# The first and the last of 64 recurrent steps rearranged: one segment's preparation between dense heads, stores in 4 KB runs, other queues, and output weights that stay in their slots

## The chip, the cores and the metric

The kernel runs on one core of a Trainium2 chip. The core has a matrix engine (TensorE, PE in the profile; PEld are its weight loads), a vector engine (DVE), a scalar engine (ACT), GpSimd (POOL) and a sync engine (SP) that does nothing here but issue DMAs. On-chip memory (SBUF) has 128 partitions; matmuls write to PSUM. The metric is device time of one execution in microseconds (us), lower is better. 16 DMA engines move all data between DRAM and SBUF; DMAs are issued on queues by SP, ACT and POOL.

## The reference

Two branches work on one layer-normalised input; their sum and the input make the output. All arrays are bfloat16.

```python
xn = _layernorm(x)                                   # x: 1 x 2048 x 1024
# branch A: memory-augmented recurrent attention, 64 segments of 32 rows, 32 heads of 128
mem = mem0                                           # 8 rows
for s in range(64):
    h = concat([mem, xn[:, 32*s:32*(s+1)]])          # 40 rows
    q, k, v = h @ Wq, h @ Wk, h @ Wv                 # each 1024 x 4096
    scores = where(mask, q @ k.T * scale, -1e9)      # per head, 40 x 40
    o = softmax(scores) @ v @ Wo                     # 4096 x 1024
    mem = o[:, :8]                                   # goes into the next segment
    outs.append(o[:, 8:])
# branch B: the two rows of xn with the largest xn @ w_r go through a gated MLP (F = 3584)
y = silu(x_sel @ w_gate) * (x_sel @ w_up) @ w_down * sigmoid(r_sel)
return x + concat(outs) + (xn + scatter(y))
```

The rows that carry memory make the 64 segments a chain: segment s+1 cannot begin before the output projection of segment s has given its 8 rows.

## The kernel before

**Split of the rows.** Each segment has 24 rows on which the next segment's memory depends, together with the 8 memory rows, and 8 rows that nothing waits for in the chain, called the left rows. The chain handles 32 rows per step (24 of x and 8 of memory). The left rows of all segments, 512 in all, have their q, k and v computed once, in the first step, with dense matmuls (`left_qk`, `left_v`), and their output projection once, after the last step (`left_rows_out`).

**Weights.** Wq, Wk, Wv and Wo are cut into 64 granules of 512 KB. 44 are resident in SBUF, one is held in two pieces, one in spare PSUM banks, and 18 (`streamed`) are read from DRAM in every step through a pool `wstream` of 5 slots (tile name `g`). The list `flow` holds the order of all such reads; `fetch` takes its head and issues it on SP. In the first step the reads come from the weight arrays; GpSimd also copies the streamed granules to scratch DRAM (`copy_block`, tiles `wsc`), from which later steps read. A step has six phases p = 0 to 5 (q, k, q, k, v, v for two halves of the heads; `PSm`, L699), and then 16 pieces of output projection (`WO`, L735). A table `hooks` puts small work (transposes, scores, softmax, attention) at a phase and a granule, here (5, 0) for the softmax of the second half.

**The first step.** `left_qk(mat, half, ...)` runs 16 heads, each of 8 matmuls (L477) and one ACT copy into `GA` (L479); it runs behind phases 0 to 3. For the first half's q its heads 0 to 7 run before the recurrent chain starts. Then come the mean and deviation of segment 0's rows (`spread(0, 1)`: PE L254, DVE L259 to L261), their normalising (`norm_seg(0)`, DVE L289 to L304), the transposes into the step's left operand `ST` (`new_st`, `mem_to_st`: PE L309, ACT L328, DVE L333), and the statistics of all other rows (`row_stats`, DVE L241/L242, tiles t = 1 to 15). Behind phase 0, `left_done(0)` needs these for `spread(1, NT)`, again L254 on PE. The gathered q and k of a half go to DRAM (`ql_d`, L490, on POOL). `left_v` runs behind phases 4 and 5: four blocks b of 128 left rows, each with four times 8 matmuls (L499) into `PSV`; ACT and DVE alternate in copying them to one of four slices of `VG` (L502), and SP stores each slice to `vl_d` (L503). A slice is written again by the next block, so its store must be done by then. `left_done(4)` loads eight output granules into one area, `W8B` (SP, L138). `GATE` is a four-column copy on POOL whose only role is to hold back the GpSimd copies behind it.

**Between steps.** `load_qkl` (L553, POOL) reads one segment's left q and k, 128 KB, from `ql_d` to the tile `QKL`.

**The last step and after.** The projection of the left rows needs all 16 output granules again (`WOS`): 11 are resident, and `flow` ends with five entries of a step 64 that read the five streamed ones (g = 49, 52, 56, 59, 62) once more. `left_rows_out(k)` makes two blocks with 64 matmuls each (`WD`, L809). The weights of branch B (tiles `MW`, 46 loads) go into homes that the last step frees (`fetch_moe`); `after(s, g)` issues one load behind each streamed output granule, and `gate_up` (`GU`, L871) and the last matmuls (`YP`, L895) use them.

The order on every engine is the order of the code; the pools only add waits.

Of the kernel before, what the change touches and what calls it, by code (L numbers as in the profile page):

```python
# [8 lines left out]
BF16 = mybir.dt.bfloat16  # L9
# [19 lines left out]
def kernel(  # L29
# [16 lines left out]
    nc = tc.nc  # L46
# [67 lines left out]

    ql_d = [dram.tile([2, 8, P, 256], BF16, name=f"ql_d{t}") for t in range(NSEG // 8)]
    vl_d = [dram.tile([16, 16, XL, 2, P], BF16, name=f"vl_d{t}") for t in range(4)]
# [18 lines left out]

    def load_resident(g):
        t = room(g, f"wres{g}")
        nc.sync.dma_start(out=granule_out(t, g), in_=granule_dram(g))  # L138
        res_tiles[g] = t
# [64 lines left out]
    RIL = MISC[:, 892:908].bitcast(F32).rearrange("p (t c) -> p t c", c=2)  # L204
    GATE = MISC[:, 908:912]

# [41 lines left out]
    def spread(t0, t1):  # L248

        n = t1 - t0  # L250
        sd_rows(MV[:, t0:t1, :], VE[:, t0:t1])
        PD = OPB
        for s in range(4):
            nc.tensor.matmul(PD[:, 32 * s:32 * s + 2 * n], lhsT=SELM[:, s, :, :].rearrange("p r g -> p (r g)"),  # L254
                             rhs=MV[:, t0:t1, :].rearrange("p t c -> p (t c)"),
                             start=(s == 0), stop=True, skip_group_check=True)
        for s in range(4):
            mr = MR.rearrange("p (t s) c -> p t s c", s=4)[0:XR4, t0:t1, s, :]
            nc.vector.tensor_copy(out=mr, in_=PD[0:XR4, 32 * s:32 * s + 2 * n].rearrange("p (t c) -> p t c", c=2))  # L259
        nc.vector.tensor_copy(out=RI16[:, t0:t1, 0], in_=MV[:, t0:t1, 0])  # L260
        nc.vector.reciprocal(out=RI16[:, t0:t1, 1], in_=MV[:, t0:t1, 1])  # L261
# [136 lines left out]
    flow += [(s, g) for s in range(NSEG) for g in (streamed if s else first_streamed)]  # L398
    flow += [(NSEG, g) for g in streamed if g >= 48]

# [69 lines left out]
    def left_qk(mat, half, Gs, between, h0=0, h1=16):  # L470
# [13 lines left out]
        if mat == 1:  # L484
            G3 = gathered[half]
            if half == 0:
                qkl[0] = one.tile([P, 2, 2, 4, 4, XL], BF16, tag="bA", name="QKL")
            nc.vector.tensor_copy(out=qkl[0][:, half].rearrange("p m i q r -> p (m i q r)"), in_=G3[:, 0, :])
            for k in range(NSEG // 4):
                nc.gpsimd.dma_start(out=ql_d[k // 2][half, 4 * (k % 2):4 * (k % 2) + 4].rearrange("s p c -> p s c"),  # L490
                                    in_=G3[:, 4 * k:4 * (k + 1), :])

    def left_v(half, Gs):
        VG = home(hm, [P, 2048], BF16, "VG")
        for b in range(4):
            for jq in range(4):
                PSV = psA.tile([P, 512], F32, tag="acc", name="PSV")
                for kc in range(KC):
                    nc.tensor.matmul(PSV[:, :], lhsT=XLT[:, kc, P * b:P * (b + 1)], rhs=part(Gs[kc], jq),  # L499
                                     start=(kc == 0), stop=(kc == KC - 1))  # L500
                VQ = VG[:, 512 * jq:512 * (jq + 1)]
                (nc.vector.tensor_copy if jq % 2 else nc.scalar.copy)(out=VQ, in_=PSV[:, :])  # L502
                nc.sync.dma_start(out=vl_d[b][4 * jq:4 * jq + 4, :, :, half, :].rearrange("i s r e -> (s r) i e"),  # L503
                                  in_=VQ.rearrange("p (i e) -> p i e", i=4))
            if b == 1:
                if half == 0:
# [3 lines left out]
    def left_done(p):  # L510
        for g in range(8 * p, 8 * (p + 1)):
            if g in first_streamed:
                fetch()
        if p == 0:
            spread(1, NT)
            for t in range(NT):
                router_tile(t)
            nc.gpsimd.tensor_copy(out=GATE, in_=gathered[0][:, 0, 0:4])
        elif p == 1:
# [9 lines left out]
        elif p == 4:  # L529
            area("big1", [P, 8, 2048], "W8B")  # L530
            for g in AREAS["big1"]:
                load_resident(g)
        elif p == 5:
# [7 lines left out]
    def after(s, g):  # L541
# [3 lines left out]
        if s == NSEG - 1:  # L545
            if g in resident and g < 48 and g not in place and g not in resident[:3]:
                free_homes.append(g)
            if g in streamed and g >= 48:
                fetch_moe(1)

    def load_qkl(s):
        t = qkl[0] = one.tile([P, 2, 2, 4, 4, XL], BF16, tag="bA", name="QKL")
        nc.gpsimd.dma_start(out=t.rearrange("p h m i q r -> p h (m i q r)"),  # L553
                            in_=ql_d[s // 8][:, s % 8].rearrange("h p c -> p h c"))

# [7 lines left out]
    qkl = [None]  # L563
    group = {}

    left_stats()
    left_turns()
    row_stats(xt(0), S6, MV[:, 0, :])
    left_qk(0, 0, [t for _, t in first_phase], iter(()), 0, 8)
    spread(0, 1)  # L570
    norm_seg(0)
    ST = new_st(0)
    mem_to_st(OB, ST)
    for t in range(1, NT):
        row_stats(xt(t), S6, MV[:, t, :])

    for s in range(NSEG):
# [108 lines left out]
        hook(4, 6, lambda: scores(1))  # L686
        hook(5, 0, exponent)
        hook(5, 0, lambda: soften(1))
        hook(5, 4, lambda: attend(0, 0))
# [52 lines left out]
        for w in range(16):  # L742
# [4 lines left out]
            if w == 2 and s + 1 == NSEG:  # L747
                OTA = area("big0", [P, NSEG, XL * H], "OTA")
                for k in range(8):
                    load_left_out(k, nc.gpsimd)  # L750
            Gv = granule(48 + w)
            project(WO, w, Gv, lhs_main, w == 15)
            if w == 9 and s + 1 < NSEG:
# [21 lines left out]
    for k in range(8, 16):  # L775
        load_left_out(k, nc.sync)
    WOS = {g: granule(g) for g in sorted(range(48, 64), key=lambda g: g in streamed)}
    XLS = [room(resident[k], "XLS") for k in range(2)]
# [158 lines left out]
```

## Time and profile before

| | |
|---|---|
| median of 3 runs | 1912.85 us (1912.07 to 1913.66) |
| the profiled execution | 1924.64 us, its span 1923.0 us |
| granted TensorE clock, mean | 0.977 |
| busy share of the span | PE 82%, PEld 43%, DVE 47%, ACT 40%, POOL 17% |
| moved by DMA | 672.39 MB, mean 350 GB/s |

The profile is of one execution; its time is 11.8 us above the median of the unprofiled runs. A row of a timeline gives start, duration, engine, line, operation, output<-input, shapes and count, and in brackets the idle time of that engine just before it and what ended it. A row of a view of stretches gives the stretch, its length, then for each engine busy time and number of instructions, the granted clock of PE (1.00 is full), the busy share of the 16 DMA engines and GB/s. A row of DMA issues gives output<-input, the queue, the count, the size of one, and the median time from its issue to its landing.

### The profile page before, as it was taken

The page shows a single profiled execution, that of the slowest core. Times are in us where ns is not written, and L with a number is a line of the kernel's source. Part 1 is how long each engine was busy: PE and PEld are TensorE (multiplying, and loading weights), DVE is VectorE, ACT ScalarE, POOL GpSimd, SP SyncE. Part 2 cuts the span into 40 slices and gives each one's busy share as a digit, 9 for nine tenths or more (in the row PEclk, how much of TensorE's full clock was granted, in tenths as well). Part 3 has the DMA queues.
Part 4 walks back from the last instruction along what each step waited for, and adds up shares of the span by engine and source line. Part 5 has one row for each costly group of instructions (what it writes and reads, how often), then busy time and mean ns, then how long its engine had stood idle before and what let it go on. Part 6 is the DMA issues. An engine that isn't in the chain of part 4 may idle for free. (4 is left out here: it accounts for less than half of the span.)

```text
span 1923.0 us, 70950 instructions
## 1 busy us (share of the span) xinstructions
PE 1574.8 (82%) x30354; PEld 821.4 (43%) x30378; DVE 907.3 (47%) x2774; ACT 768.4 (40%) x2018; POOL 329.1 (17%) x593
## 2 busy tenths in 40 slices
PE   6898778888888778888878888888887877888778
PEld 3444334444444434444444444444444444444455
DVE  5811245445555445444545555555444445555430
ACT  2342134444444444444434444444444444444400
POOL 1042011111111111111111111111111111111200
PEclk9999989999999999999999999999999999999988
DMA  9495699999999999999999999999999999999997
GB/s 364 185 337 168 191 357 363 371 366 375 374 361 381 338 358 375 371 356 366 382 352 357 376 371 376 370 377 375 365 366 365 357 370 365 375 375 367 369 343 278
DMA packets 234173, 672.39 MB, mean 350 GB/s; under 512 B 48192, under 2 KB 55664, under 8 KB 233856
## 3 DMA queue, kind: packets, MB, share of 16 engines
q1 hardware_dynamic: 208592, 621.96, 86.6%
q0 software_dynamic: 23248, 42.22, 6.7%
q8 instruction: 237, 3.88, 0.8%
q10 hardware_dynamic: 2016, 3.67, 0.6%
q14 instruction: 80, 0.66, 0.1%
HBM read 646.74 MB, written 29.76 MB: 352 GB/s over the span
## 5 line engine op out<-in xcount | busy, mean ns | idle before, releaser
L699 PE MATMUL PSm<-wres,ST 128*32 128x512 bf16 x6400 | 543.8, 389 | 22.9 <-DVE ST L333 22.9
L699 PEld LDWEIGHTS <-ST 128*32 128x32 bf16 x12288 | 305.7, 96 | 519.3 <-issue 203.9
L699 PE MATMUL PSm<-g,ST 128*32 128x512 bf16 x3332 | 338.4, 391 | 163.5 <-DMA g<-wsc 159.7
L708 ACT CAST XB<-PSm 128x512 bf16<-128x512 f32 x256 | 150.6, 588 | 279.6 <-PE PSm L699 276.7
L735 PEld LDWEIGHTS <-OT 128*32 128x32 bf16 x8192 | 204.8, 97 | 70.5 <-issue 55.9
L553 POOL DMA_DIRECT2D QKL<-ql_d x63 | 47.0, 746 | 978.8 <-DVE OTL L669 960.1
L598 DVE COPY KT<-BT 128x512 bf16<-128x512 bf16 x128 | 53.2, 415 | 258.1 <-PE BT L588 257.7
L735 PE MATMUL WO<-W8B,OT 128*32 128x256 bf16 x4096 | 162.6, 275 | 0.0
L699 PE MATMUL PSm<-W8A,ST 128*32 128x512 bf16 x2048 | 160.4, 386 | 0.0
L735 PE MATMUL WO<-g,OT 128*32 128x256 bf16 x2560 | 133.3, 278 | 17.8 <-DMA g<-wsc 14.6
L767 POOL DMA_DIRECT2D out_dram<-XN x256 | 128.9, 514 | 83.7 <-DVE XN L765 78.0
L390 DVE COPY g<-KEPT 128x512 bf16<-128x512 bf16 x126 | 53.5, 425 | 144.6 <-PE PSm L699 133.7
L377 ACT COPY BK<-KEPT 128x512 bf16<-128x512 bf16 x126 | 78.4, 622 | 104.6 <-PE WO L735 104.6
L716 ACT CAST VM<-PSm 128x512 bf16<-128x512 f32 x128 | 80.3, 627 | 76.6 <-PE PSm L699 76.6
L593 ACT COPY QT<-BT 128x512 bf16<-128x512 bf16 x128 | 75.1, 587 | 80.9 <-PE BT L588 46.6
L588 PEld LDWEIGHTS <-XB 128*128 128x128 bf16 x1024 | 58.3, 98 | 108.4 <-ACT XB L708 44.6
L588 PE MATMUL BT<-IDENT,XB 128*128 128x128 bf16 x1024 | 102.4, 223 | 0.0
L477 PE MATMUL PSG<-XLT,wres 128*128 128x512 bf16 x326 | 100.3, 382 | 1.5 <-ACT XLT L235 1.1
L615 DVE TENSOR_TENSOR BS<-BS,CT 128x96 f32<-128x96 f32 (+1 forms) x256 | 59.7, 233 | 86.7 <-PE BS L608 82.3
L596 ACT COPY KT<-QKL 128x128 bf16<-128x128 bf16 x128 | 38.4, 300 | 142.9 <-PE BT L588 105.5
L630 DVE TENSOR_REDUCE DN<-BS 128x8 f32<-128x320 f32 x128 | 62.9, 491 | 66.5 <-ACT BS L625 66.5
L294 POOL DMA_DIRECT2D XN<-in_A_x_dram x64 | 34.1, 533 | 296.6 <-PE PSm L699 212.7
(176 smaller groups left out, 2460.3 us busy)
## 6 DMA issues: line engine op xcount, KB each, us to landing
g<-wsc SPq DMA_DIRECT2D x950, 512.0 KB, 6.2
g<-wsc SPq DMA_DIRECT2D x126, 256.0 KB, 5.4
g<-wsc SPq DMA_DIRECT2D x63, 384.0 KB, 5.9
ql_d<-GA POOLq DMA_DIRECT2D x32, 256.0 KB, 7.2
QKL<-ql_d POOLq DMA_DIRECT2D x63, 128.0 KB, 5.5
MW<-in_B_w_gate_dram SPq DMA_DIRECT2D x16, 448.0 KB, 8.0
MW<-in_B_w_up_dram SPq DMA_DIRECT2D x16, 448.0 KB, 6.4
MW<-in_B_w_down_dram SPq DMA_DIRECT2D x14, 512.0 KB, 8.9
```

Of the source, the lines that this page charges most:

```text
L377: copy(out=back[c], in_=KEPT_COLS[KEPT_WHOLE][c])
L390: copy(out=t[:, 512 * c:512 * (c + 1)], in_=KEPT_COLS[g][c])
L477: nc.tensor.matmul(PSG[:, :], lhsT=part(Gs[kc], h // 4)[:, P * (h % 4):P * (h % 4 + 1)], rhs=XLT[:, kc, :], start=(kc == 0), stop=(kc == K ...
L588: nc.tensor.transpose(out=PTq[:, il, :, :].rearrange("p j r -> p (j r)"), in_=XB[:, il * P:(il + 1) * P], identity=IDENT[:, :])
L593: nc.scalar.copy(out=QT[half][:, :, :], in_=pv)
L615: nc.vector.tensor_tensor(out=S4, in0=S4, in1=m, op=ALU.add)
L630: nc.vector.tensor_reduce(out=DN[:, :], in_=S8, axis=AX.X, op=ALU.add)
L699: nc.tensor.matmul(PSm[32 * jq:32 * jq + 32, :], lhsT=ST[:, kc, :], rhs=part(Gv, jq), start=(kc == 0), stop=(kc == KC - 1), tile_position= ...
L708: nc.scalar.copy(out=XB[:, :], in_=PSm[:, :])
L716: nc.scalar.copy(out=VM[half][:, :], in_=PSm[:, :])
L735: nc.tensor.matmul(PS[32 * g:32 * g + 32, 0:256], lhsT=lhs(h), rhs=Gv[:, D * hs + 256 * g:D * hs + 256 * (g + 1)], start=False, stop=(last ...
L767: nc.gpsimd.dma_start(out=out2[s * SEG:s * SEG + XM, 256 * g:256 * (g + 1)], in_=OB[32 * g:32 * g + XM, :])
```

## The change

In the first step:

- `left_qk(0, 0)` for heads 0 to 7 is cut in three: heads 0 and 1, then `spread(0, 1)` and `norm_seg(0)`, then heads 2 to 4, then the transposes into `ST` and the statistics of all other rows, then heads 5 to 7. The square root that `spread` needs (`sd_rows`) is issued ahead of its caller.
- `ql_d` is laid out with the 8 segments of a tile inside the partition, so that one store moves 4 KB per partition: 8 stores of 512 KB per half instead of 16 of 256 KB. `load_qkl` then reads pieces of 512 B that stand 4 KB apart.
- The second half's stores no longer follow its last head at once; two are issued behind each block of the first `left_v`, held back by `GATE`.
- The first `GATE`, and with it six copies to scratch DRAM, now waits for the last head of q (columns 124 to 128) instead of the first.
- `W8B` is loaded on POOL's queue instead of SP's.
- The softmax of the second half stands at (4, 7) instead of (5, 0) in this step alone.

In the last step the five streamed output granules stay in their slots and are not read again, and one load for branch B is issued behind every output granule.

```diff
-    ql_d = [dram.tile([2, 8, P, 256], BF16, name=f"ql_d{t}") for t in range(NSEG // 8)]
+    ql_d = [dram.tile([2, P, 8, 256], BF16, name=f"ql_d{t}") for t in range(NSEG // 8)]
...
-    def load_resident(g):
+    def load_resident(g, queue=nc.sync):
...
-    GATE = MISC[:, 908:912]
+    GATE = CT[:, 14:16].bitcast(BF16)
...
     def spread(t0, t1):
         n = t1 - t0
-        sd_rows(MV[:, t0:t1, :], VE[:, t0:t1])
...
-    flow += [(NSEG, g) for g in streamed if g >= 48]
...
-            for k in range(NSEG // 4):
-                nc.gpsimd.dma_start(out=ql_d[k // 2][half, 4 * (k % 2):4 * (k % 2) + 4].rearrange("s p c -> p s c"),
-                                    in_=G3[:, 4 * k:4 * (k + 1), :])
+            if half == 0:
+                for k in range(NSEG // 8):
+                    store_left(half, k)
+
+    def store_left(half, k):
+        nc.gpsimd.dma_start(out=ql_d[k][half], in_=gathered[half][:, 8 * k:8 * (k + 1), :])
...
+            if half == 0:
+                nc.gpsimd.tensor_copy(out=GATE, in_=VG[:, 1536:1540])
+                for k in range(2 * b, 2 * b + 2):
+                    store_left(1, k)
...
+            sd_rows(MV[:, 1:NT, :], VE[:, 1:NT])
             spread(1, NT)
...
-            nc.gpsimd.tensor_copy(out=GATE, in_=gathered[0][:, 0, 0:4])
+            nc.gpsimd.tensor_copy(out=GATE, in_=gathered[0][:, 0, 124:128])
...
             for g in AREAS["big1"]:
-                load_resident(g)
+                load_resident(g, nc.gpsimd)
...
-            if g in streamed and g >= 48:
+            if g >= 48:
                 fetch_moe(1)
...
-                            in_=ql_d[s // 8][:, s % 8].rearrange("h p c -> p h c"))
+                            in_=ql_d[s // 8][:, :, s % 8].rearrange("h p c -> p h c"))
...
     row_stats(xt(0), S6, MV[:, 0, :])
-    left_qk(0, 0, [t for _, t in first_phase], iter(()), 0, 8)
+    sd_rows(MV[:, 0:1, :], VE[:, 0:1])
+    left_qk(0, 0, [t for _, t in first_phase], iter(()), 0, 2)
     spread(0, 1)
     norm_seg(0)
+    left_qk(0, 0, [t for _, t in first_phase], iter(()), 2, 5)
     ST = new_st(0)
     mem_to_st(OB, ST)
     for t in range(1, NT):
         row_stats(xt(t), S6, MV[:, t, :])
+    left_qk(0, 0, [t for _, t in first_phase], iter(()), 5, 8)
...
-        hook(5, 0, exponent)
-        hook(5, 0, lambda: soften(1))
+        hook(*((5, 0) if s else (4, 7)), exponent)
+        hook(*((5, 0) if s else (4, 7)), lambda: soften(1))
...
+            if s + 1 == NSEG and 48 + w in streamed:
+                left_in_slots[48 + w] = Gv
...
-    WOS = {g: granule(g) for g in sorted(range(48, 64), key=lambda g: g in streamed)}
+    WOS = {g: res_tiles.get(g, left_in_slots.get(g)) for g in sorted(range(48, 64), key=lambda g: g in streamed)}
```

Three places in the instruction order follow. The first is ACT at the start of the first step. Before, all eight copies of heads 0 to 7 (`GA`) stand ahead of the square root (L246, the second ACTIVATE) and of the copy into `ST`:

```order
L246 ACTIVATE MISC<-MISC 128x4
L235 COPY XLT<-PX 128x8x128 x2
L479 CAST GA<-PSG 128x64x8 x8
L246 ACTIVATE MISC<-MISC 128x1
L328 COPY ST<-BT 128x2x4x24
L708 CAST XB<-PSm 128x512
```

With the change:

```order
L246 ACTIVATE MISC<-MISC 128x4
L235 COPY XLT<-PX 128x8x128 x2
L246 ACTIVATE MISC<-MISC 128x1
L477 CAST GA<-PSG 128x64x8 x5
L327 COPY ST<-BT 128x2x4x24
L477 CAST GA<-PSG 128x64x8 x3
L718 CAST XB<-PSm 128x512
```

The square root moved ahead of all heads, and the copy into `ST` ahead of the last three.

The second place is POOL from the last copy to scratch DRAM to the end of the first step. Before, 16 stores of the second half follow one another, and then comes the first read of `QKL`:

```order
L395 DMA wsc_122<-in_A_Wo_dram 256x1x1024
L490 DMA ql_d_89<-GA 128x4x256 x2
L490 DMA ql_d_90<-GA 128x4x256 x2
L490 DMA ql_d_91<-GA 128x4x256 x2
L490 DMA ql_d_92<-GA 128x4x256 x2
L490 DMA ql_d_93<-GA 128x4x256 x2
L490 DMA ql_d_94<-GA 128x4x256 x2
L490 DMA ql_d_95<-GA 128x4x256 x2
L490 DMA ql_d_96<-GA 128x4x256 x2
L553 DMA QKL<-ql_d_89 128x2x256
```

With the change (from the second block of `left_v` on; `CT<-VG` is `GATE`):

```order
L507 COPY CT<-VG 128x4
L492 DMA ql_d_91<-GA 128x2048
L492 DMA ql_d_92<-GA 128x2048
L507 COPY CT<-VG 128x4
L492 DMA ql_d_93<-GA 128x2048
L492 DMA ql_d_94<-GA 128x2048
L507 COPY CT<-VG 128x4
L492 DMA ql_d_95<-GA 128x2048
L492 DMA ql_d_96<-GA 128x2048
L138 DMA W8B<-in_A_Wo_dram 128x2x1024 x8
L559 DMA QKL<-ql_d_89 128x2x256
```

Each pair of stores now stands behind a copy out of `VG`, and the eight loads of `W8B` stand on POOL behind the last pair.

The third place is SP in the last step, from the last granule of step 63 (`wsc_122` is g = 62, `wsc_118` is g = 49). Before:

```order
L354 DMA g<-wsc_122 128x2048
L354 DMA g<-wsc_118 128x2048
L415 DMA MW<-in_B_w_gate_dram 128x1792
L354 DMA g<-wsc_119 128x2048
L415 DMA MW<-in_B_w_gate_dram 128x1792
L354 DMA g<-wsc_120 128x2048
L415 DMA MW<-in_B_w_gate_dram 128x1792
L354 DMA g<-wsc_121 128x2048
L415 DMA MW<-in_B_w_gate_dram 128x1792
L354 DMA g<-wsc_122 128x2048
L415 DMA MW<-in_B_w_gate_dram 128x1792 x12
L415 DMA MW<-in_B_w_up_dram 128x1792 x6
```

With the change:

```order
L353 DMA g<-wsc_120 128x2048
L353 DMA g<-wsc_121 128x2048
L353 DMA g<-wsc_122 128x2048
L413 DMA MW<-in_B_w_gate_dram 128x1792 x16
L413 DMA MW<-in_B_w_up_dram 128x1792 x6
```

The five second reads are gone, and the same 22 loads for branch B follow the last granule directly.

More of the change, by code (lines that the diff above doesn't have):

```diff
@@ L134, in room @@
         return areas[tag][:, i, :]
-    def load_resident(g):
+    def load_resident(g, queue=nc.sync):
         t = room(g, f"wres{g}")
-        nc.sync.dma_start(out=granule_out(t, g), in_=granule_dram(g))
+        queue.dma_start(out=granule_out(t, g), in_=granule_dram(g))
         res_tiles[g] = t
@@ L564 @@
     group = {}
+    left_in_slots = {}
     left_stats()
```

## The prediction

> **What bounds the kernel now.** I read the page first, then the view of stretches, then the timeline of the first step engine by engine, and last the waits and DMA issues there and after the last step.
>
> ```profile
> span 1923.0 us, 70950 instructions
> DMA  9495699999999999999999999999999999999997
> DMA 28%; PE 16%; ACT 2%; DVE 2%; issue 1%; ACTq 0%; SPq 0%; DVEq 0%
> L699 PE MATMUL PSm<-g,ST 128*32 128x512 bf16 x3332 | 338.4, 391 | 163.5 <-DMA g<-wsc 159.7
> 25.00:45.00 20.00, 16.24 (x99) 7.01 (x99) 8.79 (x27) 4.85 (x11) 0.54 (x2) 0.91 1.03 395
> 300.00:1800.00 1500.00, 1229.93 (x26846) 640.53 (x26839) 756.25 (x2396) 664.86 (x1799) 262.18 (x475) 0.99 0.98 368
> ```
>
> From 300 to 1800 us the DMA engines are 98% busy at 368 GB/s, and the chain that ended last is mostly `g<-wsc`: the 63 steps after the first run at the speed at which streamed granules arrive. In the digits of DMA (one slice is 48 us) only the first step has gaps, in its second, fourth and fifth slice. So the first step is bound by something else, the chain of the recurrence begins behind it, and each microsecond that it ends earlier moves all that follows. What bounds it shows in its rows:
>
> ```profile
> 28.13 0.59 ACT L479 CAST GA<-PSG 128x512 bf16<-128x512 f32 x1 [1.14 <-PE PSG L477]
> 29.86 0.59 ACT L479 CAST GA<-PSG 128x512 bf16<-128x512 f32 x1 [1.14 <-PE PSG L477]
> 34.06 0.24 PE L254 MATMUL BT<-MISC 128*128 128x2 bf16 x4 [0.78 <-ACT MISC L246]
> 34.33 0.76 DVE L259 COPY BS<-BT 96x2 f32<-96x2 f32 x4 [16.14 <-PE BT L254]
> 36.47 0.28 PE L309 MATMUL BT<-IDENT,XN 128*128 128x128 bf16 x2 [2.17 <-DVE XN L304]
> 36.79 0.32 ACT L328 COPY ST<-BT 128x192 bf16<-128x192 bf16 x1 [2.79 <-PE BT L309]
> 37.65 1.27 DVE L241 BATCH_NORM_STATS2 MISC<-XP 128x6 f32<-128x512 bf16 x2
> 56.22 0.39 PE L370 MATMUL KEPT<-IDENT,XK 128*128 128x128 bf16 x4
> 61.36 0.18 DVE L245 TENSOR_SCALAR MISC<-MISC 128x15 bf16<-128x15 bf16 x1
> 61.84 0.27 PE L254 MATMUL BT<-MISC 128*128 128x30 bf16 x4 [5.23 <-ACT MISC L246]
> 62.00:64.00 2.00, 2.00 (x22) 0.59 (x20) 1.64 (x8) 0.00 (x0) 0.00 (x0) 0.50 1.02 410
> 64.00:66.00 2.00, 2.00 (x21) 0.80 (x21) 1.93 (x4) 0.77 (x2) 0.00 (x0) 0.73 1.03 420
> ```
>
> DVE stands idle for 16.14 us until PE has made eight heads, one each 1.73 us (29.86 less 28.13). Then 15 tiles of statistics keep it busy from 37.65 to 61.36, and PE, done at 56.6, waits 5.23 us for their result. After that wait PE's granted clock is 0.50 for two microseconds and 0.73 for two more.
>
> **Term 1, preparation between heads.** With the change L254 stands behind head 1 and the transposes behind head 4. PE comes to the transposes at the time of head 4's copy, 28.13, plus 0.24 for L254. ACT first makes that copy (0.59); from the start of L328 to the first statistics the old order took 37.65 - 36.79 = 0.86. So they start at 28.13 + 0.24 + 0.59 + 0.86 = 29.8, that is 7.8 earlier, and if nothing else holds DVE, L245 comes at 53.5 and L254 at 54.0. PE saves its waits of 0.78 and 2.17 and is there at 56.6 - 2.95 = 53.7 at the latest, so DVE still ends last, but by under 2 us. Whether the clock falls after so short a wait, a later row tells: after 3.54 us it did not (183 to 185, below). I take 2 x 0.50 + 2 x 0.27 = 1.5 as saved too. Sum: 7.8 + 1.5 = 9.3. What could hold DVE is x: its last 512 KB are issued here, and the view of the tile `XP` gives the landing.
>
> ```profile
> 34.46 0.92 SPq L208 DMA_DIRECT2D XP<-in_A_x_dram  x1
> DMA to landing us min/median/max: 6.2/12.6/18.5
> ```
>
> Their statistics would begin at 29.8 + 13 x 1.58 = 50.3 (one tile takes (61.36 - 37.65) / 15 = 1.58). At the median x is there at 34.46 + 0.92 + 12.6 = 48.0; at the longest at 53.9, 3.6 late, and the clock's 1.5 would then be lost with it. Bounds: 4.2 and 9.3. The six copies to scratch DRAM that now wait for head 15 leave the queues in these microseconds, which speaks for the median. They are needed one step later only.
>
> **Term 2, the first `left_v`.** Eight matmuls take 1.73 us, so the four slices of `VG` come round in 6.9 us.
>
> ```profile
> 161.60 0.50 DVE L621 TENSOR_TENSOR BS<-BS,NM 128x320 f32<-128x320 f32 x1
> 162.32 0.59 ACT L502 CAST VG<-PSV 128x512 bf16<-128x512 f32 x1 [1.26 <-PE PSV L499]
> 172.15 0.59 PE L499 MATMUL PSV<-W8A,XLT 128*128 128x512 bf16 x2 [1.29 <-ACT VG L502]
> 182.75 0.59 PE L499 MATMUL PSV<-W8A,XLT 128*128 128x512 bf16 x2 [3.54 <-ACT VG L502]
> 183.00:185.00 2.00, 2.00 (x11) 0.94 (x10) 0.27 (x1) 0.28 (x1) 0.00 (x0) 1.00 0.59 133
> 192.11 0.43 ACT L625 ACTIVATE BS<-BS 128x320 f32<-128x320 f32 x1
> 195.28 0.22 PE L658 MATMUL BS<-PT,VL 32*128 32x160 bf16 x1 [0.81 <-DVE PL L637]
> ql_d<-GA POOLq DMA_DIRECT2D x16, 256.0 KB, 7.3
> vl_d<-VG SPq DMA_DIRECT2D x10, 128.0 KB, 8.2
> vl_d<-VG SPq DMA_DIRECT2D x22, 128.0 KB, 2.0
> 96.00:108.00 12.00, 11.89 (x118) 5.82 (x109) 2.14 (x6) 4.72 (x9) 11.27 (x16) 1.00 0.98 277
> ```
>
> The DMA issues of 155 to 185 us show why PE waited 1.29 + 3.54 = 4.83: beside the 16 stores of `ql_d` a store of `VG` lands in 8.2 us, more than the 6.9 that it has; in 185 to 240 the median is 2.0. With the change 1 MB of `ql_d` follows each block. Runs of 512 B went at 277 GB/s (96 to 108, the first half's stores); for 4 KB runs I take the 395 of the loads at 25 to 45, since their rows are as long, so 2.7 us in each 6.9. A store of `VG` then lands in at most 2.0 + 2.7 = 4.7, in time: 4.83 saved. The softmax moved to (4, 7) makes ACT do the exponential before it frees `PSm`: 161.60 + 0.50 + 0.43 + 0.59 (copy) = 163.1, while PE needs the buffer at 162.3, so 0.8 is lost; the wait of 0.81 before L658 goes. Behind the exponential on ACT stand that copy and the first `VG` copy, and DVE has the softmax before its first slice, both inside the same 0.8. Sum: 4.83 - 0.8 + 0.81 = 4.8. Bounds: 0, if the stores collide as before, and 5.6.
>
> **Term 3, the second `left_v`.**
>
> ```profile
> 195.77 6.37 SPq L138 DMA_DIRECT2D W8B<-in_A_Wo_dram  x8
> 213.15 1.01 PE L499 MATMUL PSV<-W8A,XLT 128*128 128x512 bf16 x2 [5.58 <-ACT VG L502]
> 213.00:216.00 3.00, 2.63 (x6) 0.99 (x7) 0.68 (x1) 0.10 (x1) 0.00 (x0) 0.50 0.41 93
> 216.00:219.00 3.00, 3.00 (x9) 1.09 (x8) 0.00 (x0) 0.59 (x1) 0.00 (x0) 0.55 0.21 46
> ```
>
> Here 4 MB of `W8B` stand on SP's queue ahead of the stores of `VG`. PE waits 5.58 us and then runs 6 us at 0.50 and 0.55, another 3 x 0.50 + 3 x 0.45 = 2.8: 8.4 lost. On POOL's queue `W8B` no longer stands ahead of them but runs beside them, for 4.19 MB / 395 = 10.6 us. The nearest row is the 4.83 that `ql_d` cost beside the same stores with as many bytes at 277 GB/s; by the time it takes that is 4.83 x 277 / 395 = 3.4, and waits of that size left the clock alone. Saved: 8.4 - 3.4 = 5.0. Bounds: 0 and 8.4. Behind `W8B` on POOL stands only the first read of `QKL`; the loads have the 27.7 us of `left_v` before the projection needs them, so they cover themselves.
>
> **Term 4, the end.**
>
> ```profile
> 1845.27 1.02 PE L809 MATMUL WD<-g,OTA 128*128 128x512 bf16 x4 [1.31 <-DMA g<-wsc]
> 1847.61 1.02 PE L809 MATMUL WD<-g,OTA 128*128 128x512 bf16 x4 [1.32 <-DMA g<-wsc]
> 1874.10 2.35 PE L871 MATMUL GU<-T,MW 128*128 128x2 bf16 x82 [1.93 <-issue]
> 1912.14 4.65 PE L895 MATMUL YP<-MW,T 128*2 128x256 bf16 x112 [2.21 <-DVE YP L889]
> ```
>
> Only two waits after step 63 are for a granule read again: 1.31 + 1.32 = 2.6. The later ones are for DVE, or for nothing that the profile shows, so PE's own work sets the end, and branch B's loads, which come five granules earlier, are not what it waits for. Bounds: 0, and 2.62 MB / 395 = 6.6 if the DMA queue set the end after all.
>
> **Nothing in 63 steps** is the last term: their instructions stay, and only `QKL` is read in another order.
>
> Sum: 9.3 + 4.8 + 5.0 + 2.6 = 21.7. The profiled execution would go from 1924.64 to 1902.9. The median of the unprofiled runs stands 11.8 below that execution; I take the same 21.7 off it: 1912.85 - 21.7 = 1891.2.
>
> **The rivals.**
>
> *`W8B` is in the way on any queue.* The 16 DMA engines are shared, and the 8.2 us beside `ql_d` on POOL's queue show that a store on SP's queue suffers from the other one. If the second `left_v` still loses its 8.4, term 3 is 0: 16.7 saved, 1896.2. Against it: `ql_d` cost 4.83 and no fall of the clock. The Trainium skill, page "DMA: Bandwidth & Descriptors", section "Issuing engines are not separate DMA queues", says just this: DMAs of all issuing engines end on the same 16 engines, and another engine saves only the time of the issue. By that rule moving `W8B` gains nothing; the two landings, 8.2 and 2.0, agree with it in part. Chance 0.17.
>
> *x lands late.* Term 1 at its lower bound, 4.2: 16.6 saved, 1896.3. For it: 18.5 us was seen. Against it: six copies fewer in that time. Chance 0.10.
>
> *Slower: the read of `QKL` in pieces 4 KB apart.*
>
> ```profile
> QKL<-ql_d POOLq DMA_DIRECT2D x60, 128.0 KB, 5.5
> ```
>
> Each of 63 steps reads 131 KB this way from memory that is already busy. At 395 GB/s that takes 0.33 us. At the 277 of the short runs it is 0.47, 8.9 us in all, my bound for this term. The sum turns to slower by over 0.2% when a step loses (21.7 + 3.8) / 63 = 0.40 us, so when these bytes move at 131 / 0.73 = 180 GB/s or less. At half of 277 a step loses 0.62: 39 in all, 1930. No row shows reads of this kind; the pieces were 512 B on the SBUF side already. The Trainium skill, same page, section "Latency and other measured facts", gives copies at a row pitch of 512 KiB nearly the full rate and a fall only from 2 MiB on; by it a pitch of 4 KB would cost nothing, and no run here shows it. Chance 0.08.
>
> *Little comes of it.* All four terms at their lower bounds give 4.2, 1908.7, and with a hundredth of a microsecond per step for `QKL` less than a measurement can tell. Chance 0.05.
>
> **How the numbers follow.** The forecast, all four terms near their value, has 0.60, and it gives the time: 1891.2. Low end: terms 3 and 4 at their upper bounds, 21.7 + 3.4 + 4.0 = 29.1, so 1884. High end: both of the first rivals and nothing from term 4, 21.7 - 5.0 - 5.1 - 2.6 = 9.0, so 1904. A measurement of this kernel can tell 0.2%, 3.8 us, from no change. Faster by more: 0.60 + 0.17 + 0.10 = 0.87; within: 0.05; slower: 0.08.
>
> **What would show it.** Right: the second L254 (new L253) near 54 with a wait under 2 us and the clock at 1.00 behind it; no wait of L499 for `VG` in the first `left_v`; one or two short ones in the second; no `g<-wsc` among the waits of L809; steps of unchanged length between 300 and 1800 us. Wrong: the first step not ending some 19 us earlier, a wait of the first projection for `W8B`, or longer steps, which would point to `QKL`.

## The result, and the profile after

| | before | after |
|---|---|---|
| median | 1914.58 us (20 runs, 1905.08 to 1924.73) | 1902.09 us (20 runs, 1883.63 to 1924.28) |
| ratio | | 0.9922, 95% interval 0.9898 to 0.9947: 14.9 us less, 10.1 to 19.5 |
| the profiled execution | 1924.64 us, span 1923.0 | 1890.66 us, span 1889.0 |

The change makes the kernel faster, by 0.8%. The ratio leaves out four runs of after that lie over 1.5% above its fastest (1913.52 to 1924.28 us); with all 20, the medians of the table are 12.5 us apart. The two profiled executions are 34.0 us apart, more than twice that, so the first question is what of these 34 belongs to the change. The cast that ends a step (`XN<-WO`, 64 times) cuts the span into three stretches. Its group in the view of the tile `XN` gives the first and the last start, of before and then of after:

```profile
L765 DVE CAST XN<-WO x64: 423/425/426, 246.4 to 1829.1; 128x256 bf16<-128x256 f32 x64
```

```profile
L777 DVE CAST XN<-WO x64: 423/425/426, 229.6 to 1798.8; 128x256 bf16<-128x256 f32 x64
```

The first step ends 16.8 us earlier. The next 63 steps take 1569.2 instead of 1582.7, which is 13.5 less. From the last cast to the end it takes 90.2 instead of 93.9. The page and the view of stretches of after, lines that answer to the first ones of the prediction:

```profile
span 1889.0 us, 70934 instructions
DMA  9676799999999999999999999999999999999995
DMA 30%; PE 14%; DVE 2%; ACT 2%; issue 1%; ACTq 0%; SPq 0%; DVEq 0%
L709 PE MATMUL PSm<-g,ST 128*32 128x512 bf16 x3332 | 335.7, 388 | 151.0 <-DMA g<-wsc 147.4
300.00:1800.00 1500.00, 1234.31 (x26981) 642.81 (x26980) 757.40 (x2400) 664.82 (x1804) 271.38 (x489) 0.99 0.99 371
```

The picture is the same: only the first step has gaps in DMA, and behind it the streamed granules set the time. They came at 371 GB/s here and at 368 before. Whether that difference is the change's, the experiments have to say. The first step of after, from the timelines of PE, DVE and POOL and the view of stretches:

```profile
51.47 0.18 DVE L245 TENSOR_SCALAR MISC<-MISC 128x15 bf16<-128x15 bf16 x1
51.95 0.25 PE L253 MATMUL BT<-MISC 128*128 128x30 bf16 x4 [2.12 <-ACT MISC L246]
53.71 0.62 PE L709 MATMUL PSm<-g,ST 128*32 128x512 bf16 x4
55.54 0.61 PE L475 MATMUL PSG<-XLT,g 128*128 128x512 bf16 x1
153.58 0.59 PE L500 MATMUL PSV<-W8A,XLT 128*128 128x512 bf16 x2 [0.94 <-ACT VM L726]
188.28 5.80 POOL L138 DMA_DIRECT2D W8B<-in_A_Wo_dram  x8 [6.50 <-DMA ql_d<-GA]
202.69 0.59 PE L500 MATMUL PSV<-W8A,XLT 128*128 128x512 bf16 x2 [4.44 <-DVE VG L503]
202.00:205.00 3.00, 2.31 (x8) 0.96 (x8) 0.64 (x1) 0.38 (x1) 0.00 (x0) 0.75 0.93 245
205.00:208.00 3.00, 3.00 (x11) 1.13 (x10) 0.69 (x1) 0.21 (x1) 0.00 (x0) 0.68 0.40 91
```

The second L253 comes 10 us earlier behind a wait of 2.12 in place of 5.23. In the first `left_v` no wait for `VG` is left, only the 0.94 that the earlier exponential costs. In the second one wait of 4.44 is left, and the clock falls behind it. The end, from the timelines of PE and ACT:

```profile
1833.11 0.18 PE L863 MATMUL PSG<-T 1*128 1x1 bf16 x1 [5.23 <-DVE T L861]
1824.72 6.61 ACTq L828 DMA_DIRECT2D out_dram<-XLS  x2
1831.36 1.28 ACT L855 ACT_TABLE_LOAD   x1 [11.78 <-DMA out_dram<-XLS]
1832.66 0.20 ACT L855 ACTIVATE T<-CT 1x2 bf16<-1x2 f32 x1
```

The two waits for a granule are gone, but the wait ahead of `PSG` is 5.23. In before it was 3.24:

```profile
1865.97 0.17 PE L851 MATMUL PSG<-T 1*128 1x1 bf16 x1 [3.24 <-DVE T L849]
```

### The profile page after: what moved, and what is told of

The parts are those of the page before. It is cut to its first block, busy times and chain, and to the rows that moved or that the text cites. A ratio compares the mean times of both kernels' runs of the same rounds, so it can differ in the third digit from the quotient of the medians.

```text
span 1889.0 us, 70934 instructions
## 1 busy us (share of the span) xinstructions
PE 1565.8 (83%) x30353; PEld 818.8 (43%) x30378; DVE 906.6 (48%) x2774; ACT 766.7 (41%) x2018; POOL 320.1 (17%) x589
## 5 line engine op out<-in xcount | busy, mean ns | idle before, releaser
L709 PE MATMUL PSm<-g,ST 128*32 128x512 bf16 x3332 | 335.7, 388 | 151.0 <-DMA g<-wsc 147.4
L293 POOL DMA_DIRECT2D XN<-in_A_x_dram x64 | 34.1, 533 | 296.4 <-PE PSm L709 204.8
```

Source lines behind the costliest of these rows:

```text
L709: nc.tensor.matmul(PSm[32 * jq:32 * jq + 32, :], lhsT=ST[:, kc, :], rhs=part(Gv, jq), start=(kc == 0), stop=(kc == KC - 1), tile_position= ...
```

## The experiments

One table serves all. It has the start of the third phase (the first `PSm` row behind 80 us), the length of both `left_v` (from the start of the first `PSV` row to the end of the last), the stretch from the third phase's start to the first step's cast, the 63 steps, and the end. Each row is one profile, in us.

| kernel | third phase | first / second `left_v` | to the cast | 63 steps | end |
|---|---|---|---|---|---|
| before | 95.42 | 32.9 / 36.0 | 151.0 | 1582.7 | 93.9 |
| before, again (e11) | 95.48 | 32.7 / 34.2 | 148.4 | 1565.1 | 94.8 |
| before + heads (e1) | 87.06 | 37.0 / 33.6 | 152.5 | 1575.8 | 95.9 |
| before + end (e2) | 96.87 | 33.8 / 33.7 | 149.7 | 1576.3 | 94.9 |
| after | 85.83 | 28.9 / 34.1 | 143.8 | 1569.2 | 90.2 |
| after, again (e12) | 88.62 | 28.9 / 33.0 | 142.6 | 1568.4 | 94.2 |
| after, old layout (e3) | 88.65 | 28.9 / 33.1 | 142.8 | 1571.6 | 94.4 |
| after, `W8B` on SP (e4) | 86.11 | 28.9 / 39.5 | 148.9 | 1586.5 | 93.0 |
| after, stores at once (e5) | 87.13 | 37.6 / 27.8 | 146.2 | 1577.9 | 92.2 |
| after, `W8B` behind the quarters (e6) | 88.34 | 28.9 / 27.8 | 139.9 | 1579.4 | 90.4 |
| after, sigmoid first (e7) | 84.87 | 28.9 / 35.0 | 144.6 | 1572.6 | 85.2 |
| after, spread later (e8) | 83.99 | 28.9 / 32.7 | 142.3 | 1580.9 | 92.4 |
| after, three edits (e9) | 83.81 | 28.9 / 27.8 | 137.9 | 1568.0 | 85.9 |
| after, `W8B` two by two (e10) | 88.48 | 28.9 / 27.8 | 137.6 | 1570.3 | 91.5 |

**Both kernels again.** No edit; one more profile each.

> The kernel before, unchanged, for a second profile. Theory (the stretch of the 63 later steps differs from run to run and not by the change): it lies between 1565 and 1590 us and differs from the first profile's 1582.7 by several us, while the first step from the third phase's start on (151.0 us) and the end (93.9) differ by under 2.5 us. Rival (the layout of ql_d makes the later steps shorter): 1580 to 1585 us again.

> The changed kernel, unchanged, for a second profile. Theory: the stretch of the 63 later steps lies between 1565 and 1590 us, not at 1569.2 again but for chance; the first step from the third phase's start to its last cast takes 143.8 us within 2.5, the end 90 to 94.5. Rival (the layout of ql_d makes the later steps shorter): 1567 to 1572 us again.

Before, again took 1905.48 us and after, again 1895.48. The 63 steps of the same kernel took 1582.7 and 1565.1 us. The view of stretches of the two profiles of before, the second one below, shows PE just as busy and the DMA rate 4 GB/s apart, with 581.34 and 581.38 MB moved:

```profile
246.00:1829.00 1583.00, 1295.86 (x28230) 673.95 (x28222) 794.09 (x2513) 697.87 (x1888) 282.41 (x509) 0.99 0.98 367
```

```profile
244.00:1809.00 1565.00, 1294.12 (x28222) 672.21 (x28222) 793.55 (x2513) 696.29 (x1888) 282.50 (x509) 0.99 0.99 371
```

So the steps' length differs from run to run with the same bytes and with DMA 98% busy in both; why the transfers went faster in one of them is open. The 1568.4 of after, again would by itself fit the rival; the 1565.1 of before, again doesn't, nor the 1586.5 of e4, which has the new layout. The stretch to the cast of before differed by 2.6, where I had allowed 2.5, and the end of after by 4.0. So single profiles tell a term only from about 3 us on, and the means below are taken over all kernels that share a stretch.

**The old layout in the changed kernel (e3).** `ql_d` as `[2, 8, P, 256]`, stores and reads to match.

```diff
-    ql_d = [dram.tile([2, P, 8, 256], BF16, ...
+    ql_d = [dram.tile([2, 8, P, 256], BF16, ...
...
```

> The changed kernel with the left q and k stored as the kernel before stores them in the memory (512-byte runs, one step's columns together), still in 16 stores of 512 KB at the changed places. Theory (the layout costs the steps nothing, and the 13.5 us by which the 63 later steps are shorter in the changed kernel's profile than in the profile of before come from the run, not from the change): the stretch from the cast that ends step 0 to the one that ends step 63 lies between 1562 and 1590 us whatever the layout, the ratio is that of the changed kernel (0.992) within 0.0025; stores of 1024 short packets land later than 5.2 us, and one or two waits of the first left_v for VG may come back, 0 to 3.5 us. Rival A (the strided read of QKL slows the steps and takes part of the gain): here the time is 5 to 9 us below the changed kernel's, ratio 0.988 to 0.990. Rival B (the 4 KB runs themselves make the steps shorter): 13 us above the changed kernel's, ratio 0.999.

Measured: median 1897.03, ratio 0.9921 (0.9886 to 0.9955), that of the changed kernel. Over all kernels the 63 steps take 1574.3 us with the old layout (mean of five) and 1574.8 with the new one (mean of nine). Both rivals fall: neither do the 4 KB runs shorten a step nor does the strided read lengthen it, as far as means of profiles that lie between 1565 and 1587 us can tell. The view of DMA issues gives the landing of `QKL`, of e3 and then of after:

```profile
QKL<-ql_d POOLq DMA_DIRECT2D x59, 128.0 KB, 5.4
```

```profile
QKL<-ql_d POOLq DMA_DIRECT2D x59, 128.0 KB, 5.7
```

No wait for `VG` came back in the first `left_v` either, so the layout gave nothing there: the stores' place did (e5, below, takes it back).

**The heads alone (e1) and the end alone (e2).** Before, with one part of the change each.

```diff
...
-    left_qk(0, 0, ..., 0, 8)
+    sd_rows(MV[:, 0:1, :], VE[:, 0:1])
+    left_qk(0, 0, ..., 0, 2)
     spread(0, 1)
     norm_seg(0)
+    left_qk(0, 0, ..., 2, 5)
...
+    left_qk(0, 0, ..., 5, 8)
```

> The kernel before with one part of the change: the preparation of step 0 between the dense heads (heads 0 to 1, spread, norm_seg, heads 2 to 4, mem_to_st and the row statistics, heads 5 to 7), and sd_rows ahead of them. Theory (the shift is kept to the end of the step): the matmuls of the left rows' heads behind the first phase resume at about 56.4 us instead of 65.69, the third phase starts at about 86 instead of 95.41, and the cast that ends the first step comes at 237.1 instead of 246.39; time 9.3 us below the kernel before, ratio 0.995. Rival (what is gained early is lost again to loads that come no earlier, in the third to sixth phase or at the first projection): the phases start 9 us earlier, but the cast that ends the step comes after 243; ratio 0.998 or more. The other steps and the end are as in the kernel before under both.

Median 1903.98, ratio 0.993 (0.9904 to 0.9956). The phase starts 8.4 us earlier and the cast comes at 239.6, 6.8 earlier: 2.5 later than expected, of which 1.5 are in the stretch to the cast. The first `left_v` is 4.1 longer than in before, since PE's clock was 0.50 from 173 to 179 us, from within a wait of 4.03 for `VG` on; the second one is 2.4 shorter. The theory holds, not the rival's "after 243".

```diff
-    flow += [(NSEG, g) for g in streamed if g >= 48]
...
-            if g in streamed and g >= 48:
+            if g >= 48:
                 fetch_moe(1)
...
+            if s + 1 == NSEG and 48 + w in streamed:
+                left_in_slots[48 + w] = Gv
...
-    WOS = {g: granule(g) for g in ...
+    WOS = {g: res_tiles.get(g, left_in_slots.get(g)) for g in ...
```

> The kernel before with one part of the change: the last step's output granules stay in their slots, and an expert load is issued behind every granule of the last projection. Theory: the first step ends at 246.4 as before; the two waits of the left rows' projection for a streamed granule (1.31 and 1.32 us) are gone, and from the cast that ends step 63 to the end it takes 91.3 instead of 93.9 us; ratio 0.9986. Rival (the 3.7 us by which that stretch is shorter in the changed kernel are not these two waits but other waits, or differ from run to run): the two waits are gone, and the stretch is still 93 to 95 us. Second rival (the expert loads, issued earlier, fill the queues beside the last projection): the last step itself grows by 2 us or more.

Median 1910.0, ratio 0.9982 (0.9955 to 1.0008), too wide to tell. The profile tells more: the waits of the projection for `g` are gone, and the end still takes 94.9, as the first rival says. The next wait has taken their place; the timeline of PE in e2:

```profile
1861.35 0.18 PE L853 MATMUL PSG<-T 1*128 1x1 bf16 x1 [6.88 <-DVE T L851]
```

In both profiles of before it was 3.24. The nine profiles with the changed end and the sigmoid in its old place have 5.14 to 6.88.

**The sigmoid first (e7).** In the lines of ACT above, the sigmoid on which `PSG` waits stands behind the two stores of `XLS` and a table load of 1.28. In before, the second store goes as soon as DVE has made the second block's sums:

```profile
1862.28 1.28 DVE L815 TENSOR_TENSOR XLS<-XLS,WD 128x512 bf16<-128x512 bf16 x2 [4.29 <-PE WD L809]
1863.59 0.60 ACTq L816 DMA_DIRECT2D out_dram<-XLS  x1
```

In after, the sums are ready at 1828.70 and the second store goes at 1830.76. The chain that ended last puts the first store's way to the memory between them (first row from DVE's timeline, the others from that chain):

```profile
1827.42 1.28 DVE L827 TENSOR_TENSOR XLS<-XLS,WD 128x512 bf16<-128x512 bf16 x2 [2.73 <-PE WD L821]
1824.72 5.95 DMA out_dram<-XLS
1830.76 0.58 ACTq L828
```

The second store goes within 0.04 us of its sums in the three profiles with the old end, and 2.0 to 3.7 us behind them in the nine with the changed one. So with PE's two waits gone, the landing of the first store became the wait that ends last on this path. The sigmoid's inputs are ready since the first step.

```diff
+    nc.scalar.activation(out=SIGR, in_=V8[:, 0:2], func=ACTF.Sigmoid)   # and SIG4
     row_stats(XS, s6, mv[:, 0, :])
...
     left_rows_out(0)     # now with the transposes of XNS in its second block
-    nc.scalar.activation(out=SIGR, in_=V8[:, 0:2], func=ACTF.Sigmoid)   # and SIG4
```

> The changed kernel with the routed rows' sigmoid, its row SIG4 and the zeroing ahead of the statistics of the end (they were behind the first half of the left rows' output), and the eight transposes of the two routed rows in the second quarter of the left rows' projection. Theory (the waits for streamed granules that the change removed at the end came back in front of PSG, where PE waits for DVE, which waits for ScalarE's sigmoid behind a store of XLS): the wait of 5.2 us ahead of PSG is gone, no other over 1 us takes its place, and from the cast that ends step 63 to the end it takes 84 to 87 us instead of 90.2 (93.0 and 94.4 in two kernels with the same end). Rival (the expert loads bound the end: PE comes earlier and waits for MW): waits for MW of 3 us or more at the GU or YP products, and 89 to 94 us.

Median 1890.98, ratio 0.9899 (0.9868 to 0.9929). The end takes 85.2 us, and 85.9 in e9, which has this edit too; the nine other profiles with the changed end have 92.6 on average. PE's timeline in e7 has no wait ahead of `PSG`, and no wait for `MW`; the 0.19 ahead of `GU` is "issue":

```profile
1832.02 0.17 PE L868 MATMUL PSG<-T 1*128 1x1 bf16 x1
1838.21 2.35 PE L888 MATMUL GU<-T,MW 128*128 128x2 bf16 x82 [0.19 <-issue]
```

So the path of the end is PE and, until this edit, that chain through ACT, not the expert loads. The sigmoid's move and that of the transposes were not run apart.

**The stores at once (e5).** All eight stores of the second half at the end of `left_qk(1, 1)`.

```diff
-            if half == 0:
-                for k in range(NSEG // 8):
-                    store_left(half, k)
+            for k in range(NSEG // 8):
+                store_left(half, k)
...
-            if half == 0:
-                nc.gpsimd.tensor_copy(out=GATE, in_=VG[:, 1536:1540])
-                for k in range(2 * b, 2 * b + 2):
-                    store_left(1, k)
```

> The changed kernel with the eight ql_d stores of the second half issued at once at the end of left_qk(1,1), as the first half's are, not two behind each quarter of the first left_v. The layout in the memory stays the changed one. Theory (the waits for VG in the first left_v come from these stores beside vl_d's): the two waits of before return, 1.29 and 3.54 us, so that the cast that ends step 0 comes at 233 to 235 instead of 229.6; W8B, which waits for these stores, may start earlier and take back part in the second left_v, up to 4.4. Rival (stores of 4 KB packets drain fast enough before the first left_v needs VG again): no wait over 0.5 us there, and the cast is at 229.6 or earlier.

Median 1902.42, ratio 0.9962 (0.9932 to 0.9993), cast at 233.3. The waits are back; the view of waits of e5 from 150 to 200 us, all in the first `left_v`:

```profile
PE PSV L499 <- DVE VG L502: 4.8, 2, 3.5
PE PSV L499 <- ACT VG L502: 3.2, 2, 2.2
```

Of the 8.0, 2.24 and 1.34 stand beside `ql_d`. The other two (3.50 and 0.96) stand beside `W8B`, which now starts at 168.80 and leaves the second `left_v` alone. Both take 65.4 us together, against 61.6 to 63.9 in the five profiles with the change's stores and `W8B` (after twice, e3, e7, e8): the placing of the stores is worth 1.5 to 3.8 us.

**`W8B` on SP (e4).** `load_resident(g)` in place of `load_resident(g, nc.gpsimd)`.

> The changed kernel with the loads of W8B back on SP's queue, ahead of the stores of the second left_v. Theory (part of the old loss was the queue: SP waits for the ql_d stores and holds up the vl_d stores behind): the second left_v loses some 8 us to waits for VG and to the clock instead of 4.4, and the cast that ends step 0 comes at 233 to 234 instead of 229.6; ratio 0.994. Rival (the bytes are in the way, whatever the queue): the waits for VG add up to 4 to 5 us as in the changed kernel, and the cast comes within 1 us of 229.6.

Median 1905.12, ratio 0.9949 (0.9918 to 0.998), cast at 235.0: the theory, and a little more. SP's timeline in e4 shows it:

```profile
188.21 3.98 SPq L138 DMA_DIRECT2D W8B<-in_A_Wo_dram  x8
192.30 17.27 SPq L504 DMA_DIRECT2D vl_d<-VG  x8
```

SP waits for the last `ql_d` store, and the second `left_v`, which began at 182.8, gets its first store out at 192.30. In after, where this `left_v` began at 182.5, it went at 185.21:

```profile
185.21 17.82 SPq L504 DMA_DIRECT2D vl_d<-VG  x8
```

PE waited 9.12 us for `VG` in e4. So POOL's queue takes away a wait that the gated stores would have made.

**`W8B` in pieces (e6, e10).** e6 loads two granules behind each quarter of the second `left_v`. e10 loads the first two ahead of it and two behind each of the first three quarters:

```diff
-            for g in AREAS["big1"]:
+            for g in AREAS["big1"][:2]:
                 load_resident(g, nc.gpsimd)
...
+            elif b < 3:
+                nc.gpsimd.tensor_copy(out=GATE, in_=VG[:, 1536:1540])
+                for g in AREAS["big1"][2 * b + 2:2 * b + 4]:
+                    load_resident(g, nc.gpsimd)
```

> The changed kernel with W8B loaded two granules at a time behind each quarter of the second left_v, instead of eight at once ahead of it. Theory (eight loads at once hold up the vl_d stores, on which VG and so PE wait): the wait of 4.44 us for VG in the second left_v falls under 1.5, the cast that ends step 0 comes at 226 to 227 instead of 229.6; the waits of the first projection for the streamed granules and W stay 6.5 us in all, since their loads are issued behind the last store. Ratio to the kernel before 0.990 to 0.991. Rival (W8B comes too late for the first projection): waits of WO for W8B of 2 to 5 us take the place, and the cast is at 229 to 231.

> The changed kernel with W8B's loads two ahead of the second left_v and two behind each of its first three quarters (in the run with two behind each of the four quarters PE waited 5.7 us for W8B in the first projection). Theory: no wait of PE over 1.5 us for VG in the second left_v and none over 1 us for W8B in the first projection; from the start of the third phase to the cast that ends step 0 it takes 139 to 140 us, against 143.8 in the changed kernel. Rival: the waits for W and the streamed granules grow by as much, 143 us.

e6: median 1898.83, ratio 0.9942 (0.9912 to 0.9972), no better than the changed kernel's; cast at 228.2. No wait for `VG` is left, but the last pair is late; theory and rival both hold in part, as the waits of e6's first projection show:

```profile
PE WO L747 <- DMA W8B<-in_A_Wo_dram: 5.7, 2, 3.4
PE WO L747 <- DMA W<-in_A_Wo_dram: 1.9, 2, 1.2
```

e10 took 1889.58 us in its one run; `left_v` runs its 27.8 without a stop, `W8B` is in time, and the stretch to the cast is 137.6.

**The spread later (e8).** The second `spread` and the router's tiles go behind the sixth granule of the second phase.

```diff
-            spread(1, NT)
-            for t in range(NT):
-                router_tile(t)
...
+        def statistics():
+            spread(1, NT)
+            for t in range(NT):
+                router_tile(t)
+        if s == 0:
+            hook(1, 5, statistics)
```

> The changed kernel with the second spread (15 tiles) and the router's tiles moved from the end of the first phase into the second phase, behind its sixth granule. Theory (PE's wait of 2.12 us for the square root, and the 2.3 us at a lower clock behind it, are the last price of the preparation): no wait of L253 over 0.3 us, the matmuls of the second phase at full clock, the heads behind it resume at 53 instead of 56.37, and the cast that ends step 0 comes 3 us earlier, at 226 to 227. Rival (VectorE's router work, now 4 us later, is in the way of the copies of the second and third phase): waits of PE for VectorE of 2 us or more there, and the cast is at 229 or later.

Median 1897.34, ratio 0.9932 (0.9906 to 0.9957). The heads resume at 53.58, the clock stays up, and the cast comes at 226.3. L253 still waits 0.76 there, now for a copy of ACT. Of the 3.3 us by which the cast is earlier than in after, 1.8 stand at the start of the third phase; most of the rest is the second `left_v` (32.7 against 34.1), which this edit does not touch. The theory holds in the profile for those 1.8; the timed ratio can't tell it from the changed kernel's 0.9922.

**All three (e9).** e7, e8 and e10 together.

> The changed kernel with three further edits together: the sigmoid and the routed rows' turn moved as in e7, the second spread and the router's tiles moved as in e8, and W8B's loads two ahead of the second left_v and two behind each of its first three quarters. Theory (the three gains lie in different stretches and add up): the cast that ends step 0 at 221 to 224 instead of 229.6 (3 us for the spread, 3 to 4 for VG), from the cast that ends step 63 to the end 85 to 87 us; ratio to the kernel before 0.984 to 0.987, 7 to 11 us below the changed kernel with the sigmoid moved alone. Rival (the first projection waits for its last loads, which are issued behind the last store, whatever comes earlier): the waits of WO grow by what left_v gains, the cast at 225 to 227, ratio 0.987 to 0.990.

Median 1883.53, ratio 0.9852 (0.9807 to 0.9897), with its cast at 221.7 and an end of 85.9. The gains add up, and this version has the lowest ratio, though its interval overlaps that of e7. Of its waits from 150 to 222 us these are the longest:

```profile
PE WO L753 <- DMA W<-in_A_Wo_dram: 4.1, 2, 3.3
PE WO L753 <- DMA g<-in_A_Wo_dram: 2.2, 1, 2.2
```

They are what is left: loads that are issued behind the last store of `left_v`.

## Why the prediction was right, point by point

The forecast was a gain of 21.7 us. The terms as the stretches show them add up to 17.9 (8.7 + 6.1 + 0.8 + 2.3), and the timed difference is 14.9 (10.1 to 19.5). The time, 1902.09, lies in the stated range, but 1.9 us from its high end and 10.9 from the 1891.2 that was given. Terms 1, 2 and 4 came, each with one step wrong; term 3 hardly came. That is the case of the first rival (16.7 us, chance 0.17) rather than that of the forecast.

- **Term 1 (9.3): right.** The third phase starts at 95.9 in the three profiles with the old order and at 87.2 in the nine that have only the change's heads: 8.7. L253 was put at 54.0; it stood between 51.95 and 54.80. The wait is 2.12 to 2.15, not under 2. That the clock would stay at 1.00 was wrong in seven of nine: in after a group of four matmuls takes 0.62 from 53.71 on, where e7, without the fall, has 0.40. DVE never waited for x, neither in after nor in e1, where the copies to scratch DRAM stand as before. Part of the 8.7 is luck: head 0, which PE runs ahead of all that the change moves, took 1.9 us from its first matmul to its copy in six of the 14 profiles and 3.2 to 3.6 in the other eight, after and its repetition (e12) among both kinds. The same two matmuls in after and in e12:

```profile
17.92 0.59 PE L475 MATMUL PSG<-XLT,wres 128*128 128x512 bf16 x2
```

```profile
19.16 1.06 PE L475 MATMUL PSG<-XLT,wres 128*128 128x512 bf16 x2
```

  All three profiles with the old order are slow here. The five of the nine that are slow too start the third phase at 88.2, which leaves 7.7: near 7.8, with little of the 1.5 for the clock.
- **Term 2 (4.8): right, but not for its reason.** From the start of the first `left_v` to that of the second it takes 36.9, 36.4, 37.6 and 40.8 us in the four profiles with the old stores (before twice, e2, e1) and 31.8 in all with the new ones but e5: 6.1 on average, 5.1 and 4.6 in the two of before. The larger ones have a fall of the clock, which the term left out. The softmax's move gave about nothing in sum: 0.9 to 1.1 less between the two `left_v`, 0.94 more in the first. The rate of 4 KB runs, on which I had built the term, wasn't the cause. Short runs at the same places do as well (e3), and 4 KB runs issued at once bring the waits back (e5).
- **Term 3 (5.0): mis-sized, with little left.** The second `left_v` takes 36.0, 34.2, 33.7 and 33.6 with the old loads and 34.1, 33.0, 33.1, 35.0 and 32.7 with the new ones (after twice, e3, e7, e8): 0.8 less on average, and the two overlap. The scaled wait of 3.4 was near (3.34 to 4.44). The step that failed is "waits of that size left the clock alone": in after, behind the wait, the clock was 0.75 and 0.68 for 6 us, 1.7 us lost, and both together are 6.1 of the 6.3 by which this `left_v` is longer than e10's 27.8. The 8.4 that I set against it was also that one profile's; in the three other profiles it was 5.8 to 6.4. So the first rival holds nearly all of this term: on POOL's queue `W8B` is in the way too. The Trainium skill, "DMA: Bandwidth & Descriptors", section "Issuing engines are not separate DMA queues", would have given 0, and the 0.8 is close to it. Where it says that another issuing engine saves only the time of the issue, e4 shows what that can hold: 5.4 us or more, since a waiting load kept the stores behind it on SP.
- **Term 4 (2.6): the mechanism right, the step "PE's own work sets the end" wrong.** Both waits went, and the end is 2.3 shorter on average (94.9 in three profiles, 92.6 in nine), but its single values overlap. Part of it came back ahead of `PSG` (3.24 before, 5.23 in after), where the sigmoid stood behind a store that waited for another store; e7, without that order, ends in 85.2.
- **No cost in 63 steps: right,** 1574.3 against 1574.8. The rival of a slower strided read falls. The Trainium skill, "DMA: Bandwidth & Descriptors", section "Latency and other measured facts", has copies at row pitches from 512 KiB up, with nearly the full rate at 512 KiB; read on to 4 KB, of which it says nothing, that would give no cost, and the two means agree.
- **From the profile to the median.** Taking the terms off the median and not off the profiled execution was right in kind. The median of before was 1914.58 in the longer comparison, not 1912.85, and the gain smaller. Nor could three runs tell 0.2%: 20 runs of before spread over 19.7 us, and the interval of the gain is 9.4 wide.
- **Not run alone:** the later `GATE` with its six copies, and the softmax's move. No stretch above has a gain that needs them.

## What to carry to other kernels

When a wait is removed, ask which wait on that path ends next, and look for it on the engines that issue transfers in order: here the expert's sigmoid waited behind a store, and the stores of `VG` behind a load. A large load beside small stores that a buffer waits for is better cut into pieces between them, early enough for their reader (e10, not e6), than moved to another queue as a whole. Where most of a kernel runs at the memory's rate, compare two profiles stretch by stretch, with a second profile of the same kernel beside them, before a difference is given to a change.

## What was not expected of the hardware

- The same wait of 2.12 to 2.15 us in the same place was followed by a fall of PE's clock in seven profiles and by none in two (e1, e7). Nor does a somewhat longer wait decide it: in the first `left_v` the clock stayed at 1.00 behind waits of 3.54 (before), 3.27 (e11) and 3.50 (e5), and fell to 0.5 with one of 3.03 (e2) and one of 4.03 (e1). In after the fall comes 1.3 to 1.8 us behind the end of the wait (51.95 to 53.23 and 53.71), in e1 still within the wait of 4.03 (0.50 from 173.0 on; it ends at 173.94). The rows of e7 beside those of after above:

```profile
52.58 0.25 PE L253 MATMUL BT<-MISC 128*128 128x30 bf16 x4 [2.15 <-ACT MISC L246]
54.17 0.40 PE L709 MATMUL PSm<-g,ST 128*32 128x512 bf16 x4
55.15 0.39 PE L475 MATMUL PSG<-XLT,g 128*128 128x512 bf16 x1
```

  The Trainium skill, "TensorE: Matmul & The Clock Gate", section "What's actually happening", says that the activity window is free-running. That would fit a fall that differs from run to run; no run here shows the window itself.
- In e12 the matmuls of head 0 stood 0.43 us apart, in after 0.22 (rows above), while the view of stretches gives a granted clock of 1.00 from 17 to 22 us in both. What slowed them stays open.
- With the same bytes and the same instructions, 63 steps took 1565.1 and 1582.7 us, at 371 and 367 GB/s. What sets the rate in a run stays open.
